# A channel-attention and two-layer kernel on one core: batch 0's norm sums halved, a scale row carried through DRAM, and a new table of start-up loads

## The chip, the core and the metric

The kernel runs on one NeuronCore of a Trainium2 chip. Times are device microseconds (us) of one launch; they are taken on the chip, apart from the profiled execution whose trace is read below. Engines are called PE (TensorE), DVE (VectorE), ACT (ScalarE), POOL (GpSimd) and SP (SyncE, which here issues every DMA). Each engine works through its own list of instructions in order, and waits at one whose inputs or buffers are not ready.

## What is computed

For each of B = 4 batches with N = 6080 tokens and C = 256 channels, q and k are normalized along the tokens, multiplied into a 256x256 score, which goes through a softmax, and v is multiplied by the result; the 24320 rows then go through a two-layer network with d_ff = 2048.

```
qn = q / (norm(q, axis=1) + 1e-6)          # a norm per channel, over N
kn = k / (norm(k, axis=1) + 1e-6)
a  = softmax(kn.transpose(0, 2, 1) @ qn / tau)      # [B, C, C]
x  = (v @ a).reshape(B * N, 256)
h  = x @ w_in                               # [24320, 2048]
g  = where(h >= 1, h, where(h <= -1, 0, (h + 1)**2 / 4))
out = g @ w_out                             # [24320, 256]
```

## The kernel before

The products v @ a @ w_in are taken as v @ W with W = a @ w_in, so each batch first needs its own W. Work is cut into groups (b, k, i): batch b, one of 6 pairs k of token tiles (2 x 512 tokens, the last two pairs 2 x 496), and one of 8 slices i of 256 hidden columns. For a group, `h_ops` makes four 128x512 tiles of h from seven block products (a Strassen-like form; each block product is three PE matmuls, since every operand is split into a high and a low half by `mm3`), `tile_ops` turns each into g and splits it (ACT and DVE), and `o_ops` multiplies by w_out and adds up in four PSUM banks (O00 to O11) over the eight i. Batch by batch, W is made by `make_W` (batch 0) or `make_W2`, split, and written to DRAM, from which later pairs load it (`load_W`, 896 KB).

Before the first group stands a start-up, in which batch 0's Gram matrix k^T q comes from plain fp32 matmuls on chunks of up to 512 tokens (`big_chunk`, line L818 of the trace; a 128x256 product of it shows as two records). Four buffers of 1 MB, kq0_0 to kq0_3, take turns: a chunk's load can be issued only when PE and ACT are done with the chunk four before. ACT squares the same chunk (L832) in pieces of 1024 columns, and DVE adds the squares up in `acc` (the tile mh_mem, L833), 128 x 1024: two halves of 512 columns, each k's and q's 256 channels. `norm_sums` (L839) adds `acc` over the partitions by products with a column of ones. `softmax` makes norms of the sums (the square root is POOL's `pow`, L514), inverts them, brings q's scales from a column into a row that stands on all partitions (two diagonal matrices by DVE, L524, a product with ones on PE, L532, and a copy, L535), scales the Gram matrix, takes exp on ACT (L547), and transposes on PE (L556). Seven chunks of batch 1 (`EARLY`) go through the same PE code as filler in the chain's waits. In the same stretch w_in, w_out and the first pair of v are converted: `convert` loads 512 KB and runs three ACT and six DVE instructions (L405 to L421) for each of 16 slices.

Later batches' norms come from squares of a transposed copy of k and q, and their Gram matrix from split products (L452 with kqs), both spread over the batch before; `softmax(b + 1)` is placed seven groups before the batch ends, in `q == KP * FP - 7`.

Nothing of this order is written by hand. Every step is an `op` with an engine, an estimated duration, a due time and its buffers; `Order.run` plays them through and each time takes, of the operations that could start, the earliest, and among equally early ones the one that is due first. The instructions come out in that order on each engine, so due times move them. SP's list is made the same way. The table `STARTUP` holds (kind, slice, due time, chunk whose load must have been issued); `W_DUE`, `FILL`, `V1` and so on are due times of W, of the filler chunks, of v's second pair.

Of the kernel before, what the change touches and what calls it, by code (L numbers as in the profile page):

```python
# [15 lines left out]
P = 128  # L16
# [227 lines left out]
def pool_us(n):  # L244
# [13 lines left out]
    ('v', 0, -478.3, 15),  # L258
    ('out', 5, -462.9, 17),
    ('out', 0, -306.5, 11),  # L260
    ('in', 2, -105.4, 16),
    ('in', 0, -82.1, 7),
    ('in', 1, -62.6, 6),
    ('out', 1, -4.4, 16),
    ('out', 6, 123.4, 7),
    ('out', 2, 163.6, 13),
    ('out', 7, 334.1, 17),
    ('out', 3, 371.7, 3),
    ('out', 4, 467.6, 12),
)  # L270
V_SPREAD = 2.5
WARM = 8
STORE = 15
IN3 = False
WIN_DUE = 41.7
W_DUE = -16.6
FILL = 16.7
FSTEP = -0.13
FIRST = 10
V1 = -7.1  # L280
V1S = 23.8
TAU = 0
# [4 lines left out]
def channel_attention_moe(ctx: ExitStack, tc: tile.TileContext, kq, kqT, vT, tau, w_in, w_out, outT):  # L287
# [93 lines left out]
    win_dram = [dram.tile([P, 2 * WIN], U32, name=f"win_d{i}") for i in range(FP // 2)]  # L381
    w_dram = [[dram.tile([P, WSZ], U32, name=f"w_d{b}_{i}") for i in range(FP)] for b in range(B)]
# [115 lines left out]

    def softmax(b, due):
# [20 lines left out]
        d, q, s = (buf("y") for _ in range(3))  # L520
        dd = lambda: d.ap[:, :CT * P].rearrange("p (i c) -> p i c", i=CT)
        ss = lambda: s.ap.rearrange("p (i c) -> p i c", i=CT)
        for ct in range(CT):
            op("DVE", 0.25, lambda ct=ct: V.tensor_scalar(out=dd()[:, ct, :], in0=ident,  # L524
                                                         scalar1=rn()[:, CT + ct:CT + ct + 1], scalar2=None,
                                                         op0=ALU.mult), r=[c], w=[d], due=due)
        z = buf("Z")

        def scales():
            od.uneven(3)  # L530
            for ct in range(CT):
                nc.tensor.matmul(z.ap[:, ct * P:(ct + 1) * P], lhsT=ones, rhs=dd()[:, ct, :], start=True, stop=True)  # L532

        op("PE", 0.7, scales, r=[d], w=[z], due=due + 3)
        op("DVE", 0.42, lambda: V.tensor_copy(q.ap[:, :C], z.ap[:, :C]), r=[z], w=[q], due=due + 3)  # L535
# [271 lines left out]
    def big_chunk(i, b, r0, p, T):  # L807
# [17 lines left out]
        if i == 0:  # L825
            op("ACT", act_us(1024), lambda: nc.scalar.activation(acc.ap, rb.ap[:, :1024], AF.Square), r=[rb], w=[acc],
               due=due)
            return
        for t in range(0, T, 2):
            src = lambda t=t: rb.ap[:p, t * 512:t * 512 + 1024]  # L830
            sq = Buf(sq_early)
            op("ACT", act_us(1024), lambda sq=sq, src=src: nc.scalar.activation(sq.ap[:p], src(), AF.Square), r=[rb], w=[sq], due=due)  # L832
            op("DVE", dve_us(1024), lambda sq=sq: nc.vector.tensor_tensor(  # L833
                out=acc.ap[:p], in0=acc.ap[:p], in1=sq.ap[:p], op=ALU.add), r=[sq], w=[acc], due=due)

    def norm_sums():
# [20 lines left out]
    op("PE", 1.84, norm_sums, r=[acc], w=[st.pt], due=URGENT - 20, plain=True)  # L857
# [76 lines left out]
```

## Time and profile before

| | us |
|---|---|
| median of 3 runs | 2154.58 (2154.46 to 2154.76) |
| the profiled execution, own time | 2155.51 |
| span of its trace (first to last instruction) | 2153.7 |
| PE busy | 2148.7 |
| DVE, ACT busy | 1785.9, 1634.4 |

What lies around the span is 1.8 us in that execution. A busy PE is modelled from starts, so a wait of PE shows mostly as a longer step from one record's start to the next, not as idle time. An instruction's duration includes a tail that overlaps the next one; the step from start to start is what it costs its engine in a row.

### The profile page before, as it was taken

How to read it: one execution, taken by the hardware profiler on the slowest of the kernel's cores; microseconds unless marked ns; L12 is line 12 of the kernel's file. 1: busy time of each engine (PE TensorE's matmuls, PEld its weight loads, DVE VectorE, ACT ScalarE, POOL GpSimd, SP SyncE). 2: the span in 40 equal slices, each digit the busy share in tenths (PEclk: the TensorE clock that was granted, in tenths of full speed). 3: DMA queues.
4: the chain of work that ended last, by engine and by line, in shares of the span. 5: the costliest groups of instructions: out<-in, count | busy, mean ns of one | idle time of the engine just before them, and what ended most of it. 6: DMA issues, size and time to landing. Idle time of an engine off the chain costs nothing.

```text
span 2153.7 us, 27733 instructions
## 1 busy us (share of the span) xinstructions
PE 2148.7 (100%) x9949; PEld 1811.1 (84%) x9949; DVE 1785.9 (83%) x3125; ACT 1634.4 (76%) x2926; POOL 5.1 (0%) x12
## 2 busy tenths in 40 slices
PE   9999999999999999999999999999999999999999
PEld 8888888888888888888888888888888888888887
DVE  8897877888888888888888888888888878878776
ACT  7798877776788777777778877777767777766766
POOL 0000000000000000000000000000000000000000
PEclk9999999999999999999999999999999999999999
DMA  9755445454255444444425445454443432332331
GB/s 381 275 189 188 150 157 173 142 174 148 84 210 190 164 166 152 177 161 161 146 102 211 163 159 183 152 194 152 153 144 118 151 125 91 126 125 100 125 118 37
DMA packets 81467, 340.09 MB, mean 158 GB/s; under 512 B 8370, under 2 KB 16690, under 8 KB 77490
## 3 DMA queue, kind: packets, MB, share of 16 engines
q1 hardware_dynamic: 81330, 338.33, 44.3%
q8 instruction: 78, 1.28, 0.2%
q14 instruction: 59, 0.48, 0.1%
HBM read 279.84 MB, written 58.46 MB: 157 GB/s over the span
## 4 chain that ended last, share of the span: by engine, by line
PE 96%; DVE 2%; DMA 2%; ACT 1%; issue 0%; SPq 0%; DVEq 0%; ACTq 0%
PE bank L452 96%; DMA raw<-w_in 1%; DVE mh_mem L833 1%; DMA raw<-w_out 0%; DMA kq<-kq 0%; ACT u L405 0%; DVE u L415 0%; ACT u L408 0%; DVE sf_mem L575 0%; DVE u L710 0%; ACT sf_mem L832 0%; DVE w_mem L581 0%; DVE u L419 0%; DVE u L406 0%; PE bank L532 0%
## 5 line engine op out<-in xcount | busy, mean ns | idle before, releaser
L452 PE MATMUL bank<-x,wout 128*128 128x512 f32 (+1 forms) x3951 | 1012.9, 387 | 0.2 <-DVE x L714 0.2
L452 PEld LDWEIGHTS bank<-x,wout 128*128 128x128 f32 x3951 | 738.2, 188 | 143.6 <-DVE x L714 0.6
L452 PE MATMUL bank<-v,w_mem 128*128 128x512 f32 (+1 forms) x3264 | 846.5, 387 | 0.0
L452 PEld LDWEIGHTS bank<-v,w_mem 128*128 128x128 f32 x3264 | 611.8, 188 | 120.9 <-DVE u L710 0.5
L710 DVE SCALAR_TENSOR_TENSOR u<-bank,u 128x512 f32<-128x512 f32 (+1 forms) x576 | 391.8, 681 | 236.1 <-ACT u L708 235.3
L706 ACT ACTIVATE u<-bank 128x512 f32<-128x512 f32 (+1 forms) x576 | 342.9, 595 | 226.2 <-PE bank L452 214.3
L708 ACT ACTIVATE u<-u 128x512 f32<-128x512 f32 (+1 forms) x768 | 459.7, 624 | 9.4
L714 DVE TENSOR_TENSOR x<-u,x 128x512 fp32r<-128x512 f32 (+1 forms) x658 | 439.6, 681 | 11.0 <-ACT x L712 4.0
L712 ACT CAST x<-u 128x512 fp32r<-128x512 f32 (+1 forms) x363 | 224.1, 619 | 136.4 <-DVE u L710 134.9
L452 PE MATMUL bank<-x,w_mem 128*128 128x512 f32 (+1 forms) x768 | 207.4, 387 | 0.0
L452 PE MATMUL bank<-g,wout 128*128 128x512 f32 (+1 forms) x660 | 183.7, 387 | 0.0
L452 PEld LDWEIGHTS bank<-x,w_mem 128*128 128x128 f32 x768 | 144.0, 188 | 28.3
L737 DVE TENSOR_TENSOR bank<-bank,mh_mem 128x512 f32<-128x512 f32 (+1 forms) x192 | 132.3, 689 | 24.8 <-PE bank L452 23.8
L452 PEld LDWEIGHTS bank<-g,wout 128*128 128x128 f32 x660 | 123.2, 188 | 23.7
L713 DVE CAST x<-u 128x512 fp32r<-128x512 f32 (+1 forms) x295 | 123.4, 422 | 15.1 <-DVE u L710 0.5
L741 DVE TENSOR_TENSOR mh_mem<-bank,mh_mem 128x512 f32<-128x512 f32 (+1 forms) x192 | 130.8, 681 | 5.5 <-PE bank L452 0.3
L710 DVE SCALAR_TENSOR_TENSOR u<-mh_mem,u 128x512 f32<-128x512 f32 (+1 forms) x192 | 129.7, 676 | 0.4 <-ACT u L708 0.4
L706 ACT ACTIVATE u<-mh_mem 128x512 f32<-128x512 f32 (+1 forms) x192 | 118.9, 619 | 0.0
L732 ACT COPY mh_mem<-bank 128x512 f32<-128x512 f32 (+1 forms) x192 | 110.4, 575 | 6.4 <-PE bank L452 2.2
L734 ACT COPY bank<-bank 128x512 f32<-128x512 f32 (+1 forms) x192 | 110.8, 577 | 4.0 <-PE bank L452 0.5
L452 PEld LDWEIGHTS bank<-kqs 128*128 128x128 f32 (+1 forms) x696 | 91.2, 191 | 4.4
L452 PE MATMUL bank<-kqs 128*128 128x256 f32 (+1 forms) x696 | 92.6, 283 | 0.0
(98 smaller groups left out, 1262.1 us busy)
## 6 DMA issues: line engine op xcount, KB each, us to landing
w_mem<-w_d SPq DMA_DIRECT2D x160, 896.0 KB, 4.6
raw<-kqT SPq DMA_DIRECT2D x60, 512.0 KB, 5.6
w_d<-w_mem SPq DMA_DIRECT2D x32, 896.0 KB, 4.5
raw<-kq SPq DMA_DIRECT2D x55, 512.0 KB, 5.4
kq<-kq SPq DMA_DIRECT2D x18, 1024.0 KB, 8.9
raw<-vT SPq DMA_DIRECT2D x32, 512.0 KB, 6.5
win_mem<-win_d SPq DMA_DIRECT2D x12, 1024.0 KB, 4.9
outT<-y_mem SPq DMA_DIRECT2D x32, 256.0 KB, 2.2
```

Of the source, the lines that this page charges most:

```text
L452: nc.tensor.matmul(out, lhsT=lhs(a), rhs=rhs(c), start=start and m == 0, stop=stop and m == 2, skip_group_check=skip)
L706: op("ACT", act_us(n), lambda: nc.scalar.activation(us(), src(), AF.Relu, bias=0.5, scale=0.5), r=[h], w=[u], due=d_sat)
L708: op("ACT", act_us(n), lambda: nc.scalar.activation(us(), us(), AF.Square), w=[u], due=d_sq)
L710: op("DVE", dve_us(n), lambda: nc.vector.scalar_tensor_tensor(out=us(), in0=src(), scalar=1.0, in1=us(), op0=ALU.max, op1=ALU.min), r=[h], ...
L712: op("ACT", act_us(n), lambda: nc.scalar.copy(t.ap[:, 0, :n], us()), r=[u], w=[t], due=d_hi, other=("DVE", dve1_us(n), lambda: nc.vector.t ...
L713: other=("DVE", dve1_us(n), lambda: nc.vector.tensor_copy(t.ap[:, 0, :n], us())) if g >= FIRST else None)
L714: op("DVE", dve_us(n), lambda: nc.vector.tensor_tensor(out=t.ap[:, 1, :n], in0=us(), in1=f32(t.ap[:, 0, :n]), op=ALU.subtract), r=[u], w=[ ...
L732: op("ACT", act_us(n), lambda: nc.scalar.copy(m5.ap[:, :n], a.ap[:, :n]), r=[a], w=[m5], due=d - U)
L734: op("ACT", act_us(n), lambda: nc.scalar.copy(a.ap[:, :n], z.ap[:, :n]), r=[z], w=[a], due=d - U)
L737: op("DVE", dve_us(n), lambda: nc.vector.tensor_tensor(out=bb.ap[:, :n], in0=z.ap[:, :n], in1=m5.ap[:, :n], op=ALU.add), r=[z, m5], w=[bb] ...
L741: op("DVE", dve_us(n), lambda: nc.vector.tensor_tensor(out=h22.ap[:, :n], in0=z.ap[:, :n], in1=m5.ap[:, :n], op=ALU.add), r=[z, m5], w=[h2 ...
L833: op("DVE", dve_us(1024), lambda sq=sq: nc.vector.tensor_tensor(out=acc.ap[:p], in0=acc.ap[:p], in1=sq.ap[:p], op=ALU.add), r=[sq], w=[acc ...
```

## The change

In batch 0, DVE adds the two halves of `acc` (one more 128x512 add), and `norm_sums` issues four products instead of eight. Squares and their adds get a due time of their own (`SQ`). For batches 1 to 3 the diagonals, the product on PE and the copy go; SP instead writes the two columns of scales (128 x 2, 1 KB) to a DRAM row, and a second DMA reads that row onto all 128 partitions. The `STARTUP` table and the other due times have new numbers, of which the diff shows some.

```diff
-    ('v', 0, -478.3, 15),
+    ('v', 0, -561.1, 15),
-    ('in', 0, -82.1, 7),
+    ('in', 0, -157.2, 8),
...
-W_DUE = -16.6
+W_DUE = -50.1
...
+SQ = -24.0
...
+    row_dram = [dram.tile([CT, P], F32, name=f"row_d{b}") for b in range(B)]
...
+    def scale_row(b, c, q, rn, due):
+        d, z = buf("y"), buf("Z")
...
+        op("PE", 0.7, scales, r=[d], w=[z], due=due + 3)
+        op("DVE", 0.42, lambda: nc.vector.tensor_copy(q.ap[:, :C], z.ap[:, :C]), r=[z], w=[q], due=due + 3)
...
+        if b == 0:
+            scale_row(b, c, q, rn, due)
+        else:
+            row = Buf(ap=row_dram[b])
+            op("SP", 0.45, lambda: nc.sync.dma_start(out=row_dram[b].rearrange("i p -> p i"), in_=rn()[:, CT:]), r=[c],
+               w=[row], due=due, size=1024)
+            load(q, lambda: row_dram[b].rearrange("(o i) p -> o (i p)", o=1).broadcast_to([P, C]), lambda: q.ap[:, :C],
+                 due, 128 * 1024, r=[row])
...
             op("ACT", act_us(1024), lambda: nc.scalar.activation(acc.ap, rb.ap[:, :1024], AF.Square), r=[rb], w=[acc],
-               due=due)
+               due=due + SQ)
...
     def norm_sums():
         for j in range(2 * CT):
-            for h in range(2):
-                nc.tensor.matmul(st.pt.ap[:, j:j + 1], lhsT=acc.ap[:, h * 512 + j * P:h * 512 + (j + 1) * P],
-                                 rhs=ones[:, 0:1], start=(h == 0), stop=(h == 1))
+            nc.tensor.matmul(st.pt.ap[:, j:j + 1], lhsT=acc.ap[:, j * P:(j + 1) * P], rhs=ones[:, 0:1], start=True,
+                             stop=True)
...
-    op("PE", 1.84, norm_sums, r=[acc], w=[st.pt], due=URGENT - 20, plain=True)
+    op("DVE", dve_us(512), lambda: nc.vector.tensor_tensor(out=acc.ap[:, :512], in0=acc.ap[:, :512],
+                                                           in1=acc.ap[:, 512:], op=ALU.add), w=[acc], due=URGENT - 20)
+    op("PE", 0.92, norm_sums, r=[acc], w=[st.pt], due=URGENT - 20, plain=True)
```

Where instructions moved is seen in three places. The first is PE's list from the end of batch 0's Gram matrix (bank6) to the first W products (win_mem with eT); bank5 is the filler for batch 1. Before:

```order
L818 MATMUL bank6_121<-kq0_0_77 128x256 x4
L818 MATMUL bank5_120<-kq0_1_78 128x256 x2
L839 MATMUL bank7_122<-ones_63,mh_mem_82 128x1 x8
L818 MATMUL bank5_120<-kq0_1_78 128x256 x6
L818 MATMUL bank5_120<-kq0_2_79 128x256 x8
L532 MATMUL bank7_122<-y0_109,ones_63 128x128 x2
L818 MATMUL bank5_120<-kq0_3_80 128x256 x8
L818 MATMUL bank5_120<-kq0_0_77 128x256 x2
L556 MATMUL bank7_122<-ident_65,y_mem_83 128x128 x4
L818 MATMUL bank5_120<-kq0_0_77 128x256 x4
L452 MATMUL bank6_121<-win_mem_85,eT_112 128x256 x12
L452 MATMUL bank7_122<-win_mem_85,eT_112 128x256 x12
```

and now:

```order
L830 MATMUL bank6_121<-kq0_0_77 128x256 x4
L851 MATMUL bank7_122<-ones_63,mh_mem_82 128x1 x4
L830 MATMUL bank5_120<-kq0_1_78 128x256 x8
L512 MATMUL bank7_122<-y0_109,ones_63 128x128 x2
L830 MATMUL bank5_120<-kq0_2_79 128x256 x8
L830 MATMUL bank5_120<-kq0_3_80 128x256 x2
L568 MATMUL bank7_122<-ident_65,y_mem_83 128x128 x4
L830 MATMUL bank5_120<-kq0_3_80 128x256 x4
L454 MATMUL bank6_121<-win_mem_85,eT_112 128x256 x12
L454 MATMUL bank7_122<-win_mem_85,eT_112 128x256 x12
L830 MATMUL bank5_120<-kq0_3_80 128x256 x2
```

The sums (L839, now L851) now stand right behind the last chunk of batch 0, and not behind two filler products; 8 filler products instead of 14 stand between the sums and the scales (L532, now L512), 10 as before between scales and transposes (L556, now L568), 4 as before behind those. So 22 filler products stand ahead of the first W products instead of 30, and 8 come later.

The second place is DVE's list around the last add of squares (96 x 1024) and the copy of the sums into cols. Before:

```order
L419 TENSOR_SCALAR u0_103<-u0_103 128x512
L833 TENSOR_TENSOR mh_mem_82<-mh_mem_82,y_mem_83 96x1024
L421 SCALAR_TENSOR_TENSOR wout_73<-u1_104,u0_103 128x512
L419 TENSOR_SCALAR u4_107<-u4_107 128x512
L421 SCALAR_TENSOR_TENSOR wout_73<-u3_106,u2_105 128x512
L421 SCALAR_TENSOR_TENSOR wout_73<-u5_108,u4_107 128x512
L509 COPY cols0_113<-bank7_122 128x4
```

and now:

```order
L423 SCALAR_TENSOR_TENSOR wout_73<-u1_104,u0_103 128x512
L846 TENSOR_TENSOR mh_mem_82<-mh_mem_82,y_mem_83 128x1024
L846 TENSOR_TENSOR mh_mem_82<-mh_mem_82,sf_mem_84 128x1024
L846 TENSOR_TENSOR mh_mem_82<-mh_mem_82,y_mem_83 128x1024
L846 TENSOR_TENSOR mh_mem_82<-mh_mem_82,sf_mem_84 128x1024
L846 TENSOR_TENSOR mh_mem_82<-mh_mem_82,y_mem_83 96x1024
L869 TENSOR_TENSOR mh_mem_82<-mh_mem_82 128x512
L408 TENSOR_SCALAR u2_105<-u2_105 128x512
L413 TENSOR_SCALAR u3_106<-u3_106 128x512
L415 TENSOR_SCALAR u2_105<-u2_105 128x512
L527 COPY cols0_113<-bank7_122 128x4
L417 SCALAR_TENSOR_TENSOR u2_105<-raw4_101,u2_105 128x512
```

Ahead of the copy stood six finished conversions (L421 is the last instruction of each); now four stand there (L423), with three of the six DVE instructions of a fifth. Between the copy and the next step on the norms (L515, now L533) stood eight conversion instructions; now two stand there.

The third is SP's list of loads around the fourth to eighth refill of the chunk buffers. Before:

```order
L390 DMA kq0_0_77<-kq 128x2048
L390 DMA tau_sb_72<-tau 1x1
L390 DMA kq0_1_78<-kq 128x2048
L390 DMA kq0_2_79<-kq 128x2048
L390 DMA raw2_99<-w_in 128x1024
L390 DMA kq0_3_80<-kq 128x2048
L390 DMA raw3_100<-w_in 128x1024
L390 DMA raw4_101<-w_out 128x1024
L390 DMA kq0_0_77<-kq 128x2048
```

and now:

```order
L392 DMA kq0_0_77<-kq 128x2048
L392 DMA tau_sb_72<-tau 1x1
L392 DMA kq0_1_78<-kq 128x2048
L392 DMA kq0_2_79<-kq 128x2048
L392 DMA kq0_3_80<-kq 128x2048
L392 DMA kq0_0_77<-kq 128x2048
L392 DMA raw2_99<-w_in 128x1024
L392 DMA kq0_1_78<-kq 128x2048
L392 DMA raw3_100<-w_out 128x1024
```

Three conversion loads stood ahead of the second refill of kq0_0 (the last row of before); now none stands between the refills up to that one, and the first of them stands right behind it.

For the later batches, the order of the whole program shows the DVE instructions between the reciprocal of the norms and the first use of the row: 19 in batch 1, 11 each in batches 2 and 3. Over the whole program, 27 matmuls of the group products that had 512 columns now have 496 (a product next to an uneven piece of PE work is padded to 512, and there are fewer such pieces).

## Rows read from the trace of the kernel before

**Rows 1.** The page: busy time, share and instructions of each engine; and how the chain that ended last divides among engines.

```profile
PE 2148.7 (100%) x9949; PEld 1811.1 (84%) x9949; DVE 1785.9 (83%) x3125; ACT 1634.4 (76%) x2926; POOL 5.1 (0%) x12
...
PE 96%; DVE 2%; DMA 2%; ACT 1%; issue 0%; SPq 0%; DVEq 0%; ACTq 0%
```

**Rows 2.** PE in order of time, 17 to 100 us, merged: start, length, line, operation, tiles, count of records. The step to the next row is the difference of the starts.

```profile
...
17.92 30.85 PE L818 MATMUL bank<-kq 128*128 128x256 f32 x140
49.00 2.08 PE L839 MATMUL bank<-ones,mh_mem 128*128 128x1 f32 x16 [0.24 <-DVE mh_mem L833]
50.94 7.84 PE L818 MATMUL bank<-kq 128*128 128x256 f32 x28
58.62 0.61 PE L532 MATMUL bank<-y,ones 128*128 128x128 f32 x4
59.06 4.48 PE L818 MATMUL bank<-kq 128*128 128x256 f32 x20
63.38 0.60 PE L556 MATMUL bank<-ident,y_mem 128*128 128x128 f32 x4
```

**Rows 3.** Who waited for whom, PE weight loads (PEld) of the first 100 us: total, times, longest, in us.

```profile
...
PEld bank L839 <- DVE mh_mem L833: 0.6, 1, 0.6
PEld bank L452 <- DVE x L714: 0.6, 1, 0.6
PEld bank L818 <- DMA kq<-kq: 0.5, 1, 0.5
```

**Rows 4.** Single microseconds: busy time and count of PE, PEld, DVE, ACT, POOL; granted clock (1.00 is 2.4 GHz, 0.50 is 1.2 GHz); DMA share; GB/s.

```profile
31.00:32.00 1.00, 1.00 (x5) 0.54 (x3) 1.00 (x4) 0.42 (x1) 0.00 (x0) 1.00 0.98 410
51.00:52.00 1.00, 1.00 (x4) 0.82 (x4) 0.97 (x5) 1.00 (x3) 0.57 (x1) 0.50 0.95 293
53.00:54.00 1.00, 1.00 (x3) 0.80 (x3) 0.99 (x4) 0.62 (x1) 0.00 (x0) 0.50 0.90 203
```

**Rows 5.** PE in order of time, as rows 2, where the first group of output products stands.

```profile
...
87.98 0.39 PE L452 MATMUL bank<-x,wout 128*128 128x512 f32 x1
88.55 0.73 PE L452 MATMUL bank<-x,wout 128*128 128x512 f32 x2 [0.19 <-DVE x L714]
89.23 1.65 PE L452 MATMUL bank<-v,w_mem 128*128 128x512 f32 x6
90.73 0.85 PE L452 MATMUL bank<-x,wout 128*128 128x512 f32 x3
...
95.62 0.84 PE L452 MATMUL bank<-v,w_mem 128*128 128x512 f32 x3
96.30 0.84 PE L452 MATMUL bank<-x,wout 128*128 128x512 f32 x3
```

**Rows 6.** PE in order of time around batch 1's product for the scales.

```profile
...
513.62 2.14 PE L452 MATMUL bank<-x,wout 128*128 128x496 f32 x9
515.60 0.82 PE L452 MATMUL bank<-v,w_mem 128*128 128x496 f32 x3
...
518.24 0.60 PE L532 MATMUL bank<-y_mem,ones 128*128 128x128 f32 x4
518.60 0.94 PE L452 MATMUL bank<-x,w_mem 128*128 128x512 f32 x3
519.38 0.85 PE L452 MATMUL bank<-v,w_mem 128*128 128x512 f32 x3
```

**Rows 7.** DVE in order of time around the sums of batch 0.

```profile
...
47.73 1.22 DVE L833 TENSOR_TENSOR mh_mem<-mh_mem,y_mem 96x1024 f32<-96x1024 f32 x1
...
51.12 0.16 DVE L509 COPY cols<-bank 128x4 f32<-128x4 f32 x1
...
54.24 0.16 DVE L515 TENSOR_SCALAR cols<-cols 128x4 f32<-128x4 f32 x1
...
54.92 0.48 DVE L524 TENSOR_SCALAR y<-ident,cols 128x128 f32<-128x128 f32 x2
```

**Rows 8.** Longer stretches, columns as in rows 4.

```profile
51.00:60.00 9.00, 9.00 (x38) 7.73 (x38) 6.25 (x19) 3.48 (x6) 1.22 (x1) 0.83 1.00 351
60.00:160.00 100.00, 99.81 (x495) 84.68 (x494) 94.95 (x192) 89.73 (x165) 0.00 (x0) 1.00 0.63 221
```

**Rows 9.** DVE in order of time where instructions of conversions (L413, L415) stand between adds of squares (L833).

```profile
...
44.19 0.42 DVE L413 TENSOR_SCALAR u<-u 128x512 uint32<-128x512 uint32 x1
44.52 1.22 DVE L833 TENSOR_TENSOR mh_mem<-mh_mem,y_mem 128x1024 f32<-128x1024 f32 x1
45.66 0.68 DVE L415 SCALAR_TENSOR_TENSOR u<-raw,u 128x512 uint32<-128x512 uint32 x1
46.26 1.22 DVE L833 TENSOR_TENSOR mh_mem<-mh_mem,sf_mem 128x1024 f32<-128x1024 f32 x1
```

**Rows 10.** DMA issues: tiles, count, KB of each, median us from issue to landing.

```profile
...
w_mem<-w_d SPq DMA_DIRECT2D x160, 896.0 KB, 4.6
...
outT<-y_mem SPq DMA_DIRECT2D x32, 256.0 KB, 2.2
...
outT<-y_mem SPq DMA_DIRECT2D x12, 248.0 KB, 3.8
```

**Rows 11.** The tile eT (the exponentials transposed and split) in batch 1: durations in ns, first and last start in us. The last row's instruction is the one that ends it, the first the first that reads it.

```profile
...
L452 PE MATMUL bank<-win_mem,eT x12: 389/389/389, 562.2 to 568.0; 128*128 128x512 f32 x12
...
L563 DVE TENSOR_TENSOR eT<-bank,eT x1: 691/691/691, 528.6 to 528.6; 128x512 fp32r<-128x512 f32 x1
```

More of the change, by code (lines that the diff above doesn't have):

```diff
@@ L257 @@
 STARTUP = (
-    ('v', 0, -478.3, 15),
-    ('out', 5, -462.9, 17),
-    ('out', 0, -306.5, 11),
-    ('in', 2, -105.4, 16),
-    ('in', 0, -82.1, 7),
[L263 to L269, printed above, removed]
+    ('v', 0, -561.1, 15),
+    ('out', 5, -319.2, 17),
+    ('out', 0, -313.7, 9),
+    ('in', 0, -157.2, 8),
+    ('out', 1, -31.6, 17),
+    ('in', 2, 67.8, 15),
+    ('in', 1, 97.7, 13),
+    ('out', 6, 130.9, 16),
+    ('out', 2, 187.9, 14),
+    ('out', 7, 259.5, 17),
+    ('out', 4, 397.1, 14),
+    ('out', 3, 404.6, 0),
 )
-V_SPREAD = 2.5
+V_SPREAD = 11.9
 WARM = 8
-STORE = 15
+STORE = 16
 IN3 = False
-WIN_DUE = 41.7
-W_DUE = -16.6
[L277 to L282, printed above, removed]
+WIN_DUE = 172.8
+W_DUE = -50.1
+FILL = 14.8
+FSTEP = -0.37
+FIRST = 8
+V1 = -62.9
+V1S = 46.2
+TAU = -20
+SQ = -24.0
 @with_exitstack
@@ L497, in square_piece, with scales @@
            w=[rb, st.ssq], due=due)
+    def scale_row(b, c, q, rn, due):
+        d, z = buf("y"), buf("Z")
+        dd = lambda: d.ap[:, :CT * P].rearrange("p (i c) -> p i c", i=CT)
+        for ct in range(CT):
+            op("DVE", 0.25, lambda ct=ct: nc.vector.tensor_scalar(
+                out=dd()[:, ct, :], in0=ident, scalar1=rn()[:, CT + ct:CT + ct + 1], scalar2=None, op0=ALU.mult),
+               r=[c], w=[d], due=due)
+        def scales():
+            od.uneven(3)
+            for ct in range(CT):
+                nc.tensor.matmul(z.ap[:, ct * P:(ct + 1) * P], lhsT=ones, rhs=dd()[:, ct, :], start=True, stop=True)
+        op("PE", 0.7, scales, r=[d], w=[z], due=due + 3)
+        op("DVE", 0.42, lambda: nc.vector.tensor_copy(q.ap[:, :C], z.ap[:, :C]), r=[z], w=[q], due=due + 3)
     def softmax(b, due):
@@ L519, in softmax @@
         op("DVE", 0.1, lambda: V.reciprocal(rn(), nrm()), w=[c], due=due)
-        d, q, s = (buf("y") for _ in range(3))
-        dd = lambda: d.ap[:, :CT * P].rearrange("p (i c) -> p i c", i=CT)
+        q, s = buf("y"), buf("y")
         ss = lambda: s.ap.rearrange("p (i c) -> p i c", i=CT)
[L523 to L535, printed above, removed]
+        if b == 0:
[6 more added lines that the diff above has]
+                 due, 128 * 1024, r=[row])
         gm = (lambda: st.g.ap) if b else (lambda: st.g.ap.rearrange("p (i c) -> p i c", i=CT))
@@ L831, in big_chunk @@
             sq = Buf(sq_early)
-            op("ACT", act_us(1024), lambda sq=sq, src=src: nc.scalar.activation(sq.ap[:p], src(), AF.Square), r=[rb], w=[sq], due=due)
+            op("ACT", act_us(1024), lambda sq=sq, src=src: nc.scalar.activation(sq.ap[:p], src(), AF.Square), r=[rb], w=[sq],
+               due=due + SQ)
             op("DVE", dve_us(1024), lambda sq=sq: nc.vector.tensor_tensor(
-                out=acc.ap[:p], in0=acc.ap[:p], in1=sq.ap[:p], op=ALU.add), r=[sq], w=[acc], due=due)
+                out=acc.ap[:p], in0=acc.ap[:p], in1=sq.ap[:p], op=ALU.add), r=[sq], w=[acc], due=due + SQ)
     def norm_sums():
         for j in range(2 * CT):
-            for h in range(2):
-                nc.tensor.matmul(st.pt.ap[:, j:j + 1], lhsT=acc.ap[:, h * 512 + j * P:h * 512 + (j + 1) * P],
-                                 rhs=ones[:, 0:1], start=(h == 0), stop=(h == 1))
+            nc.tensor.matmul(st.pt.ap[:, j:j + 1], lhsT=acc.ap[:, j * P:(j + 1) * P], rhs=ones[:, 0:1], start=True,
+                             stop=True)
     def mark_b():
```

## Prediction, written before the changed kernel was run

> **What bounds the kernel now.** The page comes first. PE is busy for the whole span and holds 96% of the chain that ended last, DVE only 2% [rows 1]. PE's busy time is modelled, though, so I look for lost time in steps from start to start. A 512-column record steps by 0.227 us (three in 0.68) [rows 5], a 496-column one by 0.220 (nine in 1.98) [rows 6], and a record of the Gram products by 0.216 (20 in 4.32) [rows 2]. The kernel's time is then the number of PE records times these steps, plus what PE loses, plus a fixed end. So an edit pays in two ways only: fewer PE records, or fewer places where a step is too long. I find four such places, all before 91 us.
>
> Between 17.92 and 49.00 stand 140 records, 30.24 us by the step, in 31.08: 0.84 lost [rows 2]. Its two causes are weight loads that waited for a chunk of kq and for DVE's last add of squares, 0.5 and 0.6 on the load side [rows 3]. I count 0.75 for the two, and leave 0.09 to the restart behind the tau product. From 50.94 to 58.62 stand 28 records in 7.68 where 6.05 would do: 1.63 lost. The granted clock tells why: it is 0.50 there, the 1.2 GHz level, and 1.00 before [rows 4]. Ahead of the fall PE had waited for DVE and then spent 1.94 on 16 records of a single column [rows 2]. From 87.98 to 90.73 stand nine records of 0.227 in 2.75: 0.71 lost, on a wait for DVE's low half of g [rows 3, 5].
>
> **The change, part by part.** *Norm sums.* Sixteen records in 1.94 are 0.121 each [rows 2]; four products fewer are eight records, so PE saves 0.97. DVE's added 128x512 add costs 0.60, the step of another two-input instruction of that shape [rows 9]. It is hidden if DVE is early. DVE's last add began at 47.73 and took 1.14, the step of its kind [rows 7, 9], so it ended near 48.9. Ahead of it and of the sums' copy now stand four conversions and half a fifth, not six. A conversion is four instructions of 0.34 and two of 0.60 [rows 9], 2.56 in all, and 1.6 of them are 4.1. So `acc` is ready near 48.9 - 4.1 + 0.6 = 45.4. PE wants it at 49.00 less the 0.75 and the two filler products that no longer stand ahead (4 x 0.216): 47.4. The cover is 2 us; without it the 0.60 would come back.
>
> *The wait for kq.* It stood at the second refill of kq0_0, behind three conversion loads which now come later. Each is 0.52 MB, 1.28 us at the 410 GB/s seen at 31 us [rows 4], so the chunk lands 3.8 earlier against a wait of 0.5. Both waits, 0.75, go.
>
> *The clock.* Of the wait and the single-column records (0.39 + 1.94) only 0.97 is left, so I take the clock to stay up: 1.63 saved, with 0 as the other end.
>
> *Batch 0's chain.* PE starts the sums at 47.4, ends them near 48.4 and has 8 filler products (3.46) up to 51.8, where the scales stand. The copy followed PE's restart by 0.18 (50.94 to 51.12), the norms were ready for DVE 3.12 later, and the diagonals took until 55.40, another 1.16 [rows 2, 7]. That makes 52.8 and a wait of 1.0 at worst. But eight conversion instructions of DVE stood inside the 3.12, and the new list has two there. I take 0, and keep 1.0 for the range.
>
> *Scales of batches 1 to 3.* The product steps 518.24 to 518.60, and the three records behind it take 0.78 instead of 0.68 [rows 6]: 0.46 a batch, 1.38 in all. DVE loses two diagonals and a copy, which is not on the path. *Width.* 27 matmuls go from 512 to 496 columns, 0.0067 each: 0.18.
>
> *The round trip.* DVE's first use of the row waits for two DMAs in sequence, and DVE's list stands still behind it: `tile_ops` of the running group, and with that PE. The trace has no store of 4-byte pieces. The shortest DMAs in it are 256 and 248 KB stores, 2.2 and 3.8 us to landing [rows 10]. Two of them are 4.4 to 7.6. Against that stand 11 DVE instructions in batches 2 and 3 (eight of 0.60, three casts of 0.34: 5.8) and 19 in batch 1 (about 10.6). DVE is also idle for 17% of the span [rows 1], which stretches 5.8 to about 7. So the cost is 0 to 1.8 us in two batches; I take 0, since a row of 1 KB is nearer to 2.2 than to 3.8. SP too stands still between the two DMAs, but what queues behind are W loads of 4.6 us [rows 10], one a group. The chain has room: batch 1's eT was done at 529 and first read at 562 [rows 11].
>
> Here the Trainium skill speaks against the edit. Its page DMA: Bandwidth & Descriptors (Specifications) says that pieces below 512 B are slow, by a read-modify-write, and (Anatomy of one DMA) that a DMA has about 2.0 us of fixed cost; no row here shows small pieces. As an estimate from that page, with 64 packets in 0.68 us (Bandwidth), 256 pieces would add 2.7, the trip would be 6.7, and DVE would wait up to 0.9 in two batches, so that the sum below would shrink by up to 1.8.
>
> *The new plan of loads.* Here nothing is removed; work moves. 4.1 us of DVE's conversions now come behind the sums, and PE is 0.97 + 0.75 + 1.63 = 3.35 ahead, so DVE is short of 7.4 us. Its idle time before was 2.75 between 51 and 60 and 5.05 in the next 100 us [rows 8], 7.8 together: only just enough, in a stretch where it already worked 95%. What helps is that 8 filler products, 16 x 0.216 = 3.5 us, are left for later, and PE can run them while DVE catches up. The two ends are no new wait, and the whole lead of 3.35 lost again. I let one wait of the size of the old one come back, 0.8, since that is the row where DVE was late before [rows 5]; so the 0.71 of the old one may as well be called unmoved.
>
> **Sum.** Gone: 0.97 + 0.75 + 1.63 + 1.38 + 0.18 + 0.71 = 5.62. New: 0.8. Net 4.8 off the profiled execution's 2155.51, of which the span is 2153.7. Its median of three is 2154.58, 0.93 lower, so I forecast 2154.58 - 4.8 = 2149.8.
>
> **Rivals.** *The clock falls all the same.* Single-column records are still there, and a wait of PE for the scales (up to 1.0) would stand close behind. For it: in the old trace less than 3 us of such work was enough. Against: it is less than half now. Time: 2149.8 + 1.6 = 2151.4.
>
> *The round trip holds DVE.* At 3.8 a DMA each of two batches waits 1.8, and PE loses all if it has no store of finished tiles: up to 3.6, half of it likely. Time: 2151.6. It decides from 7 us for the trip on. The rule on small pieces above is the page's voice for this case.
>
> *DVE is short by more.* PE loses the lead between 60 and 100 us: 2149.8 - 0.8 + 3.35 = 2152.4.
>
> *Slower than before.* Conversions of w_out that come late hold the output products, one slice a group. If the plan pushes four more of them behind products that need them, and DVE has no idle time there, PE waits 4 x 2.56 = 10.2: 2154.58 - 5.6 + 10.2 = 2159.2. It decides from 9.9 us of such waits on. Against it: in the first 60 us only 1.6 conversions moved.
>
> *The plan changes nothing in the start-up*, because the DMA share is near 1.0 there [rows 4] and another chunk is late instead. Then only PE's work is saved, 0.97 + 1.38 + 0.18 = 2.5: 2152.1.
>
> **Chances.** Forecast 0.64 (its own range 2149.0, no new wait, to 2151.3), clock 0.12, round trip 0.09, DVE short 0.06, start-up unchanged 0.04, slower 0.05. The range goes from 2148.9 (all of 5.62) to 2152.4. A difference of 0.2% is 4.3 us, about what a measurement of this kernel tells from no change; faster than that means below 2150.3. The forecast lies only 0.5 below this line: some three quarters of its 0.64 fall under it, 0.48 of all; 0.47 stay within 0.2%, 0.05 are slower.
>
> **What would show it.** Eight records of one column in about 1 us near 47.4, with no idle step ahead; a granted clock of 1.00 from 47 to 55; the first W products near 59 instead of 65.36; no product with ones near 518; DVE's first use of the row without a wait for a DMA; steps of 0.227 between 60 and 100 us, apart from one or two. I am wrong if PE's steps there show more than 2 us lost, if the row takes over 7 us to land, or if the clock falls again.

## The result, and the profile after

The changed kernel takes 2174.84 us (median of 5 runs, 2174.22 to 2176.32) where the kernel before takes 2154.58: a ratio of 1.0095, 95% interval 1.008 to 1.011. The forecast was 2149.8 with a range up to 2152.4; it is wrong by 25 us and in its sign. The span of the profiled execution grew from 2153.7 to 2174.5, by 20.8.

The page of after: busy time of the engines, and the chain that ended last by engine.

```profile
PE 2152.6 (99%) x9929; PEld 1811.6 (83%) x9929; DVE 1785.9 (82%) x3120; ACT 1635.5 (75%) x2923; POOL 5.4 (0%) x12
PE 94%; DMA 3%; DVE 2%; ACT 0%; issue 0%; POOL 0%; SPq 0%; DVEq 0%; ACTq 0%; POOLq 0%
```

Against [rows 1] PE has 20 records less and yet 2 points less of the chain, and DMA holds 3% of the chain where it held 2%. Asked for the row's tile, the trace names who waited for its two DMAs (us, times) and how long the DMAs took from issue to landing.

```profile
  DVE y_mem L550: 16.3, 2
  DVE y L550: 2.2, 1
DMA to landing us min/median/max: 6.0/6.2/8.3
```

One place in time order, batch 2's scales: SP's issues, then DVE, then PE (start, busy, line, tiles; in brackets the idle time before and what ended it), and then the windows of the same stretch (busy us and counts of PE, weight load, DVE, ACT, POOL; PE's granted clock; DMA share; GB/s).

```profile
1022.89 0.38 SPq L544 DMA_DIRECT2D row_d<-cols  x1
1031.28 0.32 SPq L392 DMA_DIRECT2D y_mem<-row_d  x1
1031.69 0.38 SPq L392 DMA_DIRECT2D w_mem<-w_d  x1
...
1022.69 0.18 DVE L537 RECIPROCAL cols<-cols 128x4 f32<-128x4 f32 x1
...
1028.51 0.66 DVE L683 TENSOR_TENSOR v<-t,v 128x496 fp32r<-128x496 f32 x1
1037.35 0.48 DVE L550 SCALAR_TENSOR_TENSOR y_mem<-gacc,cols,y_mem 128x256 f32<-128x256 f32 x1 [8.18 <-DMA y_mem<-row_d]
...
1038.33 0.67 DVE L749 TENSOR_TENSOR bank<-bank,mh_mem 128x496 f32<-128x496 f32 x1
...
1031.08 0.82 PE L454 MATMUL bank<-x,wout 128*128 128x496 f32 x3
1039.06 2.85 PE L454 MATMUL bank<-v,w_mem 128*128 128x496 f32 x6 [7.16 <-DVE bank L749]
1041.71 1.44 PE L454 MATMUL bank<-g,wout 128*128 128x496 f32 x3
```

```profile
1024.00:1031.00 7.00, 7.00 (x33) 5.96 (x32) 5.13 (x10) 4.16 (x7) 0.00 (x0) 1.00 0.04 2
1039.00:1042.00 3.00, 2.94 (x7) 2.46 (x8) 3.00 (x7) 1.84 (x5) 0.00 (x0) 0.50 0.00 0
```

The store is issued 0.2 us behind the reciprocal and holds SP for 8.4 us; the load behind it lands 6.0 later: 14.4 us for the trip. From the store's issue DVE has 6.2 us of other work up to the row's first use (L550), and there it stands for 8.2. Behind it in DVE's list waits L749, an add of two products of h, and for that PE. While the store hangs, the DMA engines are nearly empty (share 0.04). PE stands 7.3 us, and when it restarts its granted clock is 0.50, the 1.2 GHz level: its 496-column records then step by 0.41 to 0.44 instead of 0.22, which costs about 2 us more. Batch 3 is the same (8.1 of DVE, 10.1 of PE's time); in batch 1 more work lies between, and DVE waits 2.2.

Added up by PE's steps (each record's step less the usual one of its shape), the 20.8 come from: the trip 1.7 + 9.5 + 10.1 = 21.3; a slower step of 496-column records, found later (e5), 1.9; a wait near 634 us, 0.4; fewer and narrower records -1.0 - 1.4 - 0.2; and the start-up between 15 and 200 us, where PE lost 3.52 before and loses 3.55 now. Sum 21.0.

The start-up of after, DVE, PE and ACT at the places that the prediction named:

```profile
44.42 1.23 DVE L846 TENSOR_TENSOR mh_mem<-mh_mem,sf_mem 128x1024 f32<-128x1024 f32 x1
45.75 1.22 DVE L846 TENSOR_TENSOR mh_mem<-mh_mem,y_mem 96x1024 f32<-96x1024 f32 x1
47.01 0.69 DVE L869 TENSOR_TENSOR mh_mem<-mh_mem 128x512 f32<-128x512 f32 x1
...
47.76 1.05 PE L851 MATMUL bank<-ones,mh_mem 128*128 128x1 f32 x8 [0.43 <-DVE mh_mem L869]
48.67 3.70 PE L830 MATMUL bank<-kq 128*128 128x256 f32 x16
...
58.95 3.29 PE L454 MATMUL bank<-win_mem,eT 128*128 128x256 f32 x24
...
72.97 1.66 PE L454 MATMUL bank<-v,w_mem 128*128 128x512 f32 x6 [1.52 <-ACT bank L746]
...
63.87 0.67 ACT L407 ACTIVATE u<-raw 128x512 f32<-128x512 f32 x1 [2.19 <-DMA raw<-w_in]
70.69 0.62 ACT L420 CAST win_mem<-u 128x512 fp32r<-128x512 f32 x1 [1.52 <-DVE u L417]
72.33 0.58 ACT L746 COPY bank<-bank 128x512 f32<-128x512 f32 x1
```

Eight records in 0.91, no fall of the clock behind them (16 records of the Gram products in 3.54), W's first product at 58.95, where the trace of before has it at 65.36: these went as forecast. But PE waited 0.6 for DVE's added add, and at 72.97 1.7 for an ACT copy, which stood behind a conversion, which hung on DVE, and this on a load of w_in that ACT had waited 2.19 for.

### The profile page after: what moved, and what is told of

Read it like the earlier page. It is cut to its first block, busy times and chain, and to the rows that moved or that the text cites. A ratio compares the mean times of both kernels' runs of the same rounds, so it can differ in the third digit from the quotient of the medians.

```text
span 2174.5 us, 27706 instructions
## 1 busy us (share of the span) xinstructions
PE 2152.6 (99%) x9929; PEld 1811.6 (83%) x9929; DVE 1785.9 (82%) x3120; ACT 1635.5 (75%) x2923; POOL 5.4 (0%) x12
## 4 chain that ended last, share of the span: by engine, by line
PE 94%; DMA 3%; DVE 2%; ACT 0%; issue 0%; POOL 0%; SPq 0%; DVEq 0%; ACTq 0%; POOLq 0%
PE bank L454 92%; PE bank L830 1%; DMA row_d<-cols 1%; DMA raw<-w_in 1%; DMA y_mem<-row_d 1%; DVE mh_mem L846 0%; DMA raw<-kqT 0%; DMA y<-row_d 0%; DVE x L726 0%; DVE u L722 0%; PE bank L857 0%; DVE w_mem L593 0%; DVE u L417 0%; DVE mh_mem L753 0%; DVE v L683 0%
## 5 line engine op out<-in xcount | busy, mean ns | idle before, releaser
L454 PE MATMUL bank<-v,w_mem 128*128 128x512 f32 (+1 forms) x3264 | 849.9, 389 | 16.8 <-DVE bank L749 14.2
L454 PEld LDWEIGHTS bank<-v,w_mem 128*128 128x128 f32 x3264 | 613.1, 188 | 139.8 <-DVE bank L749 15.5
L749 DVE TENSOR_TENSOR bank<-bank,mh_mem 128x512 f32<-128x512 f32 (+1 forms) x192 | 132.4, 689 | 27.1 <-PE bank L454 26.5
```

What stands on the lines that cost most here:

```text
L454: nc.tensor.matmul(out, lhsT=lhs(a), rhs=rhs(c), start=start and m == 0, stop=stop and m == 2, skip_group_check=skip)
L749: op("DVE", dve_us(n), lambda: nc.vector.tensor_tensor(out=bb.ap[:, :n], in0=z.ap[:, :n], in1=m5.ap[:, :n], op=ALU.add), r=[z, m5], w=[bb] ...
```

## Experiments

The kernel before was timed beside each run, on the same chip: 2155.0 to 2155.1. Edits are against the changed kernel where nothing else is said.

**e1: the trip undone.**

```diff
-        if b == 0:
+        if True:
             scale_row(b, c, q, rn, due)
```

> The changed kernel with one part undone: all four batches spread their scales by products with ones (batch 0's function), no trip through DRAM. Theory (the trip costs it all): PE's lost steps at 504-508 (1.7 us), 1031 (9.6) and 1573 (10.0) go, 21.3 in all, and the three products come back with 0.46 each, 1.4. That gives 2174.8 - 21.3 + 1.4 = 2154.9, so no difference from the kernel before (2154.0 to 2155.8). Rival (the new plan of loads, or the squares' priority, is to blame): 2172 to 2175, the loss stays.

2155.26, ratio 0.9999 (0.9991 to 1.0008). The theory holds: with the products back, PE loses nothing at 1031 and 1573. So the halved sums and the new plan, without the trip, gave no time that can be told from none.

**e2: the trip alone**, put into the kernel before (the `if b == 0 ... else` piece of the diff).

> The kernel before with one part of the change alone: the DRAM trip for the scales of batches 1 to 3. Theory (the trip costs it all, whatever the plan): DVE waits some 8 us at its first use of the row in batches 2 and 3, PE loses 9 to 10 us each time and 1 to 2 in batch 1, less 1.4 of products: 2154.6 + 21.3 - 1.4 = 2174.5 (2168 to 2178). Rival (the trip hurts only together with the new plan): 2153.2 to 2156.

2177.82, ratio 1.0101 (1.0085 to 1.0116). Who waited for the row, and the window of the sixteen single-column records and what follows (columns as in rows 4):

```profile
  DVE y_mem L549: 15.5, 2
...
48.00:60.00 12.00, 11.74 (x64) 10.28 (x64) 9.21 (x24) 4.92 (x7) 1.23 (x1) 1.00 0.99 355
```

DVE waits 15.5 us in two batches, PE loses 1.3 + 9.3 + 10.0. The plan of loads isn't needed for it. The 3 us above the forecast are 2.5 of the slower 496-column step (e5) and 0.8 in the start-up.

**e3: true times for the planner.** An operation gets a number `late`, added to the end that the planner reckons with.

```diff
-               w=[row], due=due, size=1024)
+               w=[row], due=due, size=1024, late=6.0)
...
-                 due, 128 * 1024, r=[row])
+                 due, 128 * 1024, r=[row], late=3.5)
```

> The changed kernel with nothing altered but two numbers that the planner reckons with: the store of the scales is taken to end 6.0 us later and the load 3.5 us later than by its own rule, which gives some 8.3 and 6.1 in all. DVE's list then has 25 instructions between the reciprocal and the first use of the row, where it had 12. Theory (the trip costs only because DVE's list stands still behind a use that is placed too early): the waits of 8 us at that use go, with them PE's losses at 1031 and 1573, and the time is 2153.5 (2152.5 to 2156). Rival (SP standing still for 14 us holds the W loads, or the trip collides with them): the wait moves to the W products, 2160 to 2175.

2155.11, ratio 1.0001 (0.9992 to 1.0010). DVE in the same place:

```profile
1020.93 0.18 DVE L538 RECIPROCAL cols<-cols 128x4 f32<-128x4 f32 x1
1036.85 0.48 DVE L551 SCALAR_TENSOR_TENSOR y_mem<-gacc,cols,y_mem 128x256 f32<-128x256 f32 x1
```

The trip still takes 14.6 us here, and SP still stands through the store, but 25 DVE instructions now lie in between where 11 did, and nothing waits: no idle time ahead of L551, PE whole at 1031 and 1573. So the rival on SP and the W loads falls, and the trip's 21.3 us came only of a use that stood too early in a list that runs in order. The time is 1.6 above the forecast, though; e5 is about that.

**e4 and e13: the DMAs by themselves.** Two short kernels with a chain of DMAs, each issued when the one ahead has landed, so that the distance of two issues is the time of the first.

```
turned[t].rearrange("i p -> p i") <- x[:, 0:2]      # 256 x 4 B, neighbours from different partitions
pairs[t] <- x[:, 0:2]                               # 128 x 8 B
near, apart <- x[:, 0:2]                            # 256 x 4 B, 64 and 512 B from piece to piece
few <- x[:16, 0:2];  one <- x[0:1, :]               # 32 x 4 B turned;  1 x 1 KB
two, four, eight, sixteen <- x[:, 0:2]              # 256 x 4 B in order, 8, 16, 32, 64 B apart
spread <- x[:, 0:2]                                 # 256 x 4 B in the turned order, 64 B apart
```

> No part of the computation: 14 kinds of DMA in a chain, each behind the landing of the one ahead, four times over, with nothing else running. Stores of the same 256 words of 4 bytes: turned as in the changed kernel (neighbours in DRAM come from different partitions); 128 pieces of 8 bytes; 4-byte pieces 64 bytes and 512 bytes apart; 32 pieces only; one piece of 1 KB. Loads: the 1 KB row into 128 partitions, and 128 rows of their own. Theory A (small pieces are slow to finish): the turned store takes about 8 us here too, half as many pieces take clearly less, one piece about 2. Rival B (in the kernel other transfers stood ahead): the turned store takes 2 to 3 us here and the spread load about 2.5 against 6.1 in the kernel. Rival C (pieces that fall into the same line of memory hinder each other): those 512 bytes apart land in 3 to 4, the turned ones in 8; likewise 128 rows of their own load faster than one row 128 times.

> No part of the computation: a chain of stores, each followed by a read of one word of what it wrote, four times over. All write the same 256 words as 4-byte pieces, in order, with 8, 16, 32 and 64 bytes from one piece to the next; then in the turned order (neighbours come from different partitions, as in the changed kernel) with 64 bytes between; then turned with none between; then 128 pairs of 8 bytes and the load of the row into 128 partitions behind them. Rival C of the first chain (pieces that fall close together in DRAM hinder each other) says: the shorter the distance the later the landing, 2 us at 64 bytes, 3 to 8 at 8 bytes; the turned order at 64 bytes takes 2 to 2.5. Its rival (the order in which the pieces are sent makes the turned store slow): the ordered stores take 2 to 2.5 at every distance, the turned order at 64 bytes takes 8 like the one without gaps.

SP's timeline of e4, second of the four rounds, and of e13, first round (start of the issue, its length, tiles):

```profile
40.00 0.37 SPq L31 DMA_DIRECT2D turned<-x  x1
48.29 0.32 SPq L32 DMA_DIRECT2D x<-turned  x1
53.12 0.32 SPq L33 DMA_DIRECT2D pairs<-x  x1
56.64 0.24 SPq L27 DMA_DIRECT2D x<-pairs  x1
58.10 0.53 SPq L35 DMA_DIRECT2D near<-x  x1
59.98 0.24 SPq L27 DMA_DIRECT2D x<-near  x1
...
70.83 0.21 SPq L41 DMA_DIRECT2D one<-x  x1
71.91 0.34 SPq L42 DMA_DIRECT2D x<-one  x1
74.78 0.34 SPq L43 DMA_DIRECT2D wide<-x  x1
```

```profile
17.09 0.41 SPq L34 DMA_DIRECT2D spread<-x  x1
18.69 0.23 SPq L27 DMA_DIRECT2D x<-spread  x1
19.82 0.39 SPq L36 DMA_DIRECT2D turned<-x  x1
27.82 0.21 SPq L27 DMA_DIRECT2D x<-turned  x1
30.93 0.35 SPq L38 DMA_DIRECT2D pairs<-x  x1
34.12 0.35 SPq L39 DMA_DIRECT2D x<-pairs  x1
```

The turned store takes 8.3 us with nothing else running (7.3 to 9.2 in eight rounds), as in the kernel: rival B falls. The same 256 pieces in the same order, 64 bytes apart, take 1.6. In order they take 3.4 to 4.8 at 8 bytes, 1.9 to 3.0 at 16, 2.2 to 2.8 at 32 and 1.9 to 2.5 at 64; pairs of 8 bytes take 2.8 to 3.5, and only 32 turned pieces still 3.0 to 4.1. So neither 256 pieces nor the turned order makes a store slow by itself; it is slow when the pieces fall close together: rival C holds. How much the order and the number add in a packed store is open, since no run stores 256 pieces of 4 bytes in order without gaps. In the packet records all 272 packets of the turned store (the 256 pieces and 16 more) have started within 1.14 us of the issue, as those of the spread one; the other 7 us pass behind the last packet's start, and the trace does not show where. It shows on the reader too: one word read behind the turned store starts 2.8 to 3.1 us after its issue, behind the spread store 0.8 to 1.1. The row's load takes 4.0 to 5.1 here behind the turned store and 2.9 to 3.1 behind the store in one piece; in the kernel 6.0, with a load of 0.9 MB issued 0.4 us behind it.

The Trainium skill, page DMA: Bandwidth & Descriptors (Anatomy of one DMA), says of DMAs that GpSimd issues that most of their fixed time of about 2.0 us goes into the receipt of the last write, not into setting up; the prediction used it for SP's DMAs. For these, which SP issues, the trace agrees that sending is the small part (1.1 of 8.3 us), but the time is not fixed: the same 256 pieces take from 1.6 to 9.2. The 512 bytes that the Trainium skill gives on that page as the least size for full rate (Specifications) do not tell these stores apart either, since all are of 4-byte pieces.

**e9: the row by pairs.** The store keeps a partition's two scales together, and DVE reads the row with a stride.

```diff
-    row_dram = [dram.tile([CT, P], F32, name=f"row_d{b}") for b in range(B)]
+    row_dram = [dram.tile([P, CT], F32, name=f"row_d{b}") for b in range(B)]
...
-            op("SP", 0.45, lambda: nc.sync.dma_start(out=row_dram[b].rearrange("i p -> p i"), in_=rn()[:, CT:]), r=[c],
+            op("SP", 0.45, lambda: nc.sync.dma_start(out=row_dram[b], in_=rn()[:, CT:]), r=[c],
...
+        qq = lambda: q.ap[:, :C].rearrange("p (i c) -> p i c" if b == 0 else "p (c i) -> p i c", i=CT)
```

> The changed kernel with the row laid out otherwise in DRAM: the two scales of a partition lie side by side, so the store has 128 pieces of 8 bytes (3.1 us to the next DMA when alone) where it had 256 of 4 bytes (8.5 alone, 8.3 in the kernel), the load brings the same 1 KB into every partition, and DVE reads it with a stride of two words. DVE's list stays as it is. Theory (pieces of a few bytes that share a line of memory are what makes the trip long): the store lands after about 3.1, the trip is 14.4 - 5.2 = 9.2 or less, DVE's wait in batches 2 and 3 falls from 8.2 to 3.0 or less, each batch regains 5.2 of PE's stall and the 2.3 of the lower clock, batch 1 its 1.7: 2174.8 - 16.7 = 2158 (2154.5 to 2160). Rival (the trip is long because the kernel's other transfers are in the way): the store lands after 8 us again, 2172 to 2175.

2157.26, ratio 1.0011 (1.0002 to 1.0020). Who waited for the row, and SP and DVE in batch 2:

```profile
  DVE y_mem L551: 2.7, 2
DMA to landing us min/median/max: 2.6/4.3/5.5
```

```profile
1020.89 0.33 SPq L544 DMA_DIRECT2D row_d<-cols  x1
1023.97 0.32 SPq L392 DMA_DIRECT2D y_mem<-row_d  x1
...
1028.26 0.48 DVE L551 SCALAR_TENSOR_TENSOR y_mem<-gacc,cols,y_mem 128x256 f32<-128x256 f32 x1 [1.09 <-DMA y_mem<-row_d]
```

With DVE's list as it was, the store lands in 2.6 to 2.8 us, the trip takes 7.4 and DVE waits 1.1 (batch 3: 7.9 and 1.6). Both kernels thus give the same cover, 7.4 - 1.1 = 6.3 and 14.4 - 8.2 = 6.2. PE loses 1.4 us to it in all instead of 21.3, and its clock stays up. The edit changes the size, number and order of the pieces together, so it shows what the layout is worth and not which of them does it.

**e5: more wide records**, on e3.

```diff
         def transposes():
-            od.uneven(3)
+            od.uneven(6)
```

> The kernel with the planner's true trip times (the run before), and one number changed: behind the transposes of eT not 3 but 6 groups of three products are left 512 columns wide where 496 would do. In that run 396 of PE's 496-column records in three stretches (519 to 561 us and the like) stepped by 224 ns instead of 220, which cost 1.7 us; in the kernel before, where 9 more records are 512 wide around the scales, only 11 did. Theory (PE falls into the slower step because fewer wide records follow a pause of the pattern): the three stretches are back at 220 and the time is 0.2 + 1.7 - 0.2 = 1.5 to 1.7 shorter, 2153.5. Rival (it is where in the group the transposes stand, not how many wide records follow): the slow stretches stay, 2155.1 to 2155.3.

2154.45, ratio 0.9996 (0.9987 to 1.0005). The question came from e3's timeline of PE: nine records from 522.91 to 524.92, 2.01 us, where nine took 1.98 before [rows 6].

```profile
522.91 2.18 PE L455 MATMUL bank<-x,wout 128*128 128x496 f32 x9
524.92 0.83 PE L455 MATMUL bank<-v,w_mem 128*128 128x496 f32 x3
```

The products' windows from 525 to 555 (PE busy and count, weight load, granted clock, DMA share, GB/s), first of e3, then of e5:

```profile
525.00:555.00 30.00, 30.00 (x136) 25.28 (x135) 1.00 0.37 139
```

```profile
525.00:555.00 30.00, 30.00 (x138) 25.60 (x137) 1.00 0.41 153
```

PE does 136 records there in e3 and 138 in e5, with no wait in either: in e3 three of four records step by 224 ns. With the wider stretch only 5 records in the whole kernel take 222 or more (401 in e3, 478 in the changed kernel, some 620 each in e2 and e9, 11 in the kernel before). So the rows bear the theory out, but two things stay open. In the kernel before, nine wide records behind the same transposes were enough, so their number alone doesn't decide; and the time fell by 0.66 where 1.5 were due, since PE lost 1.0 more in the start-up of e5's profiled execution than of e3's, with the same lists.

**e6 and e8: halved sums alone, plan alone.** e6 is the kernel before with the new `norm_sums` and the added add; e8 is e1 with the old sixteen records and without the added add.

> The kernel before with one part of the change alone: four products (8 records) for batch 0's norms behind one added DVE add. Theory, the prediction's step (PE saves 0.97, and with half the one-column records the clock stays at 1.00 behind them, 1.63): 2155.1 - 2.6 = 2152.5 as this chip's median of the kernel before stands. Rival 1 (DVE's added add is not hidden without the new order, since DVE's last add ended near 48.9 there, so PE waits 0.6 longer and the clock falls as before): 2155.1 - 0.97 + 0.6 = 2154.7. Rival 2 (the clock stays up, but PE's lead only turns into a longer wait for DVE at 60 to 90 us): 2154.1 to 2155.1.

> The kernel before with the new plan alone (numbers of the table and the squares' own priority), the sixteen one-column records and the products for the scales of all batches as before. Theory (the plan makes PE wait near 72 us for an activation that hangs on a late load of w_in, so that any lead is lost there): PE comes to that place later, by 0.97 of products and perhaps 1.63 of a lower clock, and waits that much less: 2155.0 to 2156, the same as with the halved sums (2155.3). Rival (waits and lead simply add up): 2155.3 + 0.97 + 1.63 = 2157.9, or 2156.2 if the clock stays up.

Both missed their forecasts. e6: 2160.52, ratio 1.0026 (1.0016 to 1.0037). e8: 2166.34, ratio 1.0052 (1.0039 to 1.0065). PE's timeline in e6 near 60 us, and e8's window behind its single-column records:

```profile
62.82 3.72 PE L818 MATMUL bank<-kq 128*128 128x256 f32 x16 [3.16 <-DMA kq<-kq]
```

```profile
48.90:52.90 4.00, 4.00 (x12) 3.23 (x12) 2.59 (x9) 3.73 (x5) 1.02 (x1) 0.57 1.01 402
```

In e6 the clock stays up, PE is early, and a chunk of kq is late: 3.3 us lost at 59.3 and 1.0 at 66.7. In e8, as before, sixteen records are followed by a clock of 0.57 (12 records in 4 us). But an edit of one operation also makes the planner reorder the rest of the start-up, and e8 loses 11.4 us between 58 and 200, to DVE and ACT, in a plan that fitted another list of operations. So neither run is "one part alone" in the strict sense.

**e10: stores later**, on e5.

```diff
-STORE = 16
+STORE = 18
```

> The run with the true trip times and the wide records, with one number changed: the first two stores of converted w_in (0.5 MB each) may start only two chunks of k and q later, so they no longer stand ahead of a load of w_in that was issued at 49.65 and landed near 65. In that run ACT waited 3.1 us for this load, DVE and ACT's next conversion behind it, then the copy of the h tile's bank, and for it PE, 1.7 near 72 us and 0.7 near 69. Theory (the transfers ahead of the load are what makes PE wait): 1 MB at 410 GB/s is 2.5 us, the load lands near 62.5, PE's two waits shrink by 1.5 to 2.3 in all: 2154.4 - 1.9 = 2152.5 (2152 to 2153.5). Rival (DVE is what PE waits for in the end, with some 95% of work there, so another wait takes its place): 2154 to 2156, with new idle steps of PE between 60 and 160 us.

2155.82, ratio 1.0003 (0.9994 to 1.0012): the rival. The load landed at 60.5, 4.4 earlier, and the wait at 72 was gone (first line), but others took its place at 88 and from 132 to 147 us, on DVE and ACT.

```profile
71.09 1.74 PE L455 MATMUL bank<-v,w_mem 128*128 128x512 f32 x6
...
88.42 0.73 PE L455 MATMUL bank<-x,wout 128*128 128x512 f32 x2 [0.34 <-DVE x L727]
89.38 0.97 PE L455 MATMUL bank<-v,w_mem 128*128 128x512 f32 x3 [0.24 <-ACT bank L747]
```

**e11: the trip in the old plan**, with true times and six wide groups.

> The kernel before, with its own plan and its sixteen one-column records, and the DRAM trip for the scales of batches 1 to 3, the planner's true trip times and six wide groups behind the transposes. Theory (what PE gains in the later batches is independent of the start-up): the products of the scales go, 0.46 a batch, nothing waits for the trip, no stretch of 224 ns appears: 2155.0 - 1.4 = 2153.6 (2153.2 to 2154.0). Rival (DVE, without two diagonals and a copy but with a later first use, makes PE wait at the start of the next batch, or the slow step returns): 2154.8 to 2157.

2153.89, ratio 0.9995 (0.9986 to 1.0004). The theory's size fits (1.1 of 1.4), and it is the lowest median of a kernel that does the whole computation, but its interval does not part it from the kernel before. Here, as in e2, the clock stayed at 1.00 behind the same sixteen records, which took 1.81 us; in e8 they took 1.81 too, and the clock fell. PE lost 1.5 at 60.5 to a late chunk of kq instead.

**e12: less DVE work**, on e5, lists unchanged.

```diff
-        op("DVE", 0.335, lambda: V.tensor_scalar(out=cb.ap, in0=cb.ap, scalar1=EXP_MIN, scalar2=EXP_MAX,
+        op("DVE", 0.335, lambda: V.tensor_scalar(out=cb.ap[:, :64], in0=cb.ap[:, :64], scalar1=EXP_MIN, scalar2=EXP_MAX,
```

and the mask of `mb` likewise; most of both is left out.

> The run with the true trip times and the wide records, its four engines' lists in the same order, but two of DVE's six instructions of each weight conversion work on 64 columns instead of 512 (this leaves out most of the clamping of the scale word and of its mask, so the low halves of the weights are wrong). DVE saves about 0.5 us in each of 16 conversions, some 3 us up to 72 us and 8 in all. Theory (in the first 160 us DVE is what PE waits for in the end, so every lead of PE turns into a wait): PE's waits at 47, 69 and 72 us (0.4 + 0.7 + 1.7, with the slower weight loads behind them 3.1) shrink by 1.5 to 3 us: 2154.4 - 2.2 = 2152.2 (2151.3 to 2153). Rival (the loads, or ACT's own list, set the pace there): the waits stay where they are, 2154 to 2154.8.

2153.60, ratio 0.9994 (0.9985 to 1.0003): 0.85 below e5, short of the 1.5 to 3 expected, but below the rival's 2154.0 to 2154.8. PE's loss from 15 to 200 us falls from 4.5 to 3.0: the wait at 47 goes, that at 72 shrinks from 1.7 to 1.2, that at 69 from 0.7 to 0.3. So DVE is part of what PE waits for there. The loads are another (e10 moved one and its wait went); how they share is open.

PE's loss between 15 and 200 us, summed over its steps as above:

| kernel | us |
|---|---|
| before / after | 3.5 / 3.6 |
| e1, e3, e5 (new plan, 8 records) | 4.2, 3.5, 4.5 |
| e2, e11 (old plan, 16 records) | 4.3, 4.2 |
| e10, e12 (e5 with one edit) | 5.6, 3.0 |
| e6, e8 (one part alone) | 9.3, 14.2 |

## Why the prediction was wrong

*The round trip* is the step that failed, in its price of two DMAs: "Two of them are 4.4 to 7.6", taken from stores of 248 and 256 KB [rows 10], "since a row of 1 KB is nearer to 2.2 than to 3.8". It took 14.4: 8.3 for the store and 6.1 for the load. The text said that the trace had no store of 4-byte pieces, and then priced one by its bytes. (Nor were its two rows the shortest: the trace of before has two stores of 124 KB that landed in 1.8.) The rest of the step was right: the cover of 5.8 to 7 (measured 6.2 and 6.3), the list of DVE standing still, PE behind it, the point from which it would decide ("from 7 us for the trip on"). "I am wrong if ... the row takes over 7 us to land" is what happened. The rival "the round trip holds DVE" had the mechanism, at 3.6 instead of 21.3, because it capped the trip at 7.6, thought it likely that PE loses only half (it lost 7.3 of 8.2) and did not count the lower clock at PE's restart (2.2 and 2.9 in the two batches). The range left it out: an unseen form was bounded above by the slowest row at hand. The Trainium skill's rule on pieces below 512 bytes (DMA: Bandwidth & Descriptors, Specifications) warned in the right direction, but partly by luck. The 6.7 that the prediction worked out from it was less than half the trip, and pieces of 4 bytes that lie 64 bytes apart land in 1.6.

*The eT chain's room* [rows 11] was real: e3 shows that the same trip costs nothing when its use stands later.

*Norm sums*: 0.91 us for eight records, right. DVE's added add was not hidden: the last add of squares began at 45.75, not near 44, since the adds now step by 1.33 and not 1.14, and PE waited 0.6, where a cover of 2 us was counted.

*The kq wait, the wait at 88* went as forecast. *The clock* stayed up, but its 1.63 was too large a term: it was read from one execution, 0.93 us above the median. Behind the sixteen records the clock fell in two profiled executions (before, e8) and not in two others (e2, e11). Of 81 executions of the kernel before, 36 have a mean granted clock of 0.999 and 45 of 1.000, and their medians lie 0.2 to 0.5 us apart; with the new plan and eight records (e1, e3, e5, e9, e10, e12) 3 of 65 have less than 1.000, with one of the two alone 4 of 7 (e6) and 4 of 5 (e8). So the two together keep the clock up more often, for some 0.5 us of the median at most, as an estimate from these groups. Where in an execution the clock fell, only the profiled ones show. The 2.3 net of these three terms and the new wait did not come. *The new plan* was allowed one wait of 0.8; PE lost 2.6 after 58 us. "The plan changes nothing in the start-up", a rival at 0.04, is what the steps say (3.52 and 3.55), and for its reason in part: another load was late.

*Scales of batches 1 to 3*: right by the records (twelve fewer); e11's 1.1 fits, within its noise. *Width*: 0.18 as counted, and the slower step of 1.9, which the forecast did not have, came with it.

## What to carry to other kernels

Price a DMA by the form of its pieces and where they land, not by its bytes, and a lost stretch by several executions, not by the one that was profiled; where no row shows the form, measure it in a chain of its own before a list in program order is built on it. A long trip is free if its first use stands late enough: tell the planner its true length and give it the slack that the reader has. In this start-up, with PE, DVE and the loads all near their limits, a lead of PE turned into waits for the others; what shortened it a little was work taken off DVE (e12).

## What the runs showed of the hardware

- 256 pieces of 4 bytes, stored in the turned order into one KB of DRAM with nothing else running, land after 7.3 to 9.2 us, in the same order 64 bytes apart after 1.6 (e4, e13); the packets have started within 1.15 us in both. A read behind the packed store starts some 2 us later than behind the spread one.
- PE's 496-column records fell into a step of 224 ns in three of four, for 40 us at a time, at a full granted clock and without a wait (e3); with more 512-column records behind a break only 5 did (e5). Why is open.
- After 7.2 us without work PE restarted with a granted clock of 0.50, the 1.2 GHz level. Behind the same sixteen single-column records it was 0.50 in two traces (before, e8) and 1.00 in two (e2, e11).
